# Transposing f, q and k by transfers instead of on TensorE, from the sixth unit on

**The chip, the cores and the metric.** One core of one Trainium2 chip. The metric is the device time of one execution in microseconds (us), lower is better. The median of three runs before was 474.9 us (472.83 to 475.72); later calls repeated the kernel before many times, with medians of 471.9 to 473.9. One core only, so a run counts as slow only when it is over 1.5% above the fastest of its kernel.

## The reference

A gated recurrence over 768 steps for 4 batches of 8 heads of 48 elements, then LayerNorm and a two-layer perceptron on the 384 concatenated elements. Cut to what matters:

```python
f = 1.0 / (1.0 + np.exp(-f_logit))               # q, k, v, f_logit: (4, 8, 768, 48) fp32
for t in range(S):
    state = f[:, :, t, :, None] * state + einsum('bhd,bhe->bhde', k[:, :, t], v[:, :, t])
    y[:, :, t] = einsum('bhd,bhde->bhe', q[:, :, t], state)
x = y.transpose(0, 2, 1, 3).reshape(B, S, H * D)
xn = (x - mu) / sqrt(var + 1e-6) * g_ln
out = x + maximum(xn @ w_ch1, 0.0) @ w_ch2       # 384 -> 1536 -> 384
```

## The kernel before

The 768 steps are cut into 12 units of 64. Inside a unit the recurrence becomes matrix products: f goes through a sigmoid and two running products along time (VectorE scans `after` and `upto`), k is multiplied by `after`, q by `upto`, and TensorE (PE) does the rest. The kernel runs the scans with time along the free axis, the inputs arrive with time on partitions, so f, k and q of each unit are transposed, eight 128 x 128 pieces each, on PE:

```python
def across(src, g):
    pt = one_bank(f"tr{n}")
    for a in range(NP):                                   # NP = 4, and g = 0, 1
        nc.tensor.transpose(pt[:, a * P:(a + 1) * P],
                            src[:, g, 2 * a:2 * a + 2].rearrange("p h e -> p (h e)"), ident)
    return pt.rearrange("p (s t) -> p s t", t=T)

def times(dst, pts, by):                                  # VectorE, 128 x 512 out of PSUM
    for g, pt in enumerate(pts):
        segs = slice(g * HS, (g + 1) * HS)
        nc.vector.tensor_tensor(out=dst[:, segs], in0=pt, in1=by[:, segs, 1:E1], op=ALU.mult)
...
    # do_gates, for g in 0, 1
    pt = across(loaded[n, "f"], g)
    nc.scalar.activation(out=gv[:, segs, 1:E1], in_=pt, func=AF.Sigmoid)
...
    # do_q; do_k is the same with k and "after"
    times(new("qh", [P, NS, T]), [across(loaded[n, "q"], g) for g in range(G)], at["upto"])
```

The order of all work is one string of tokens. A start-up string `START` brings in the weights and the first units; then a string `UNIT` is run for m = 3 to 11. In it `m{m}` is one piece of the perceptron of unit m (block products of 0.9 us on PE, or second-layer products of 1.95 us), `a{n}.name` a stage of the recurrence of unit n, `l{p}q` a load, `y` and `s` sums on VectorE that prepare the perceptron's products. A turn of this loop handles the perceptron of one unit and stages of three later ones:

```python
UNIT = """
a{o}.after m{m} m{m} m{m} m{m} m{m} a{n}.carried a{n}.scores a{n}.causal m{m} m{m} a{n}.chunk
a{n}.values m{m} a{n}.stats m{m} m{m} a{n}.norm m{m} m{m} m{m} m{m} m{m} s{m}
m{m} a{n}.turn a{o}.kx a{o}.k m{m} m{m} m{m} a{o}.kt a{p}.gates a{o}.upto l{p}v m{m}
l{z}f m{m} y{n} a{o}.q l{p}q a{n}.state a{o}.kept l{p}x l{p}k m{m}
"""
```

`carried`, `scores`, `chunk` and `values` matter later: each is 64 small products, which PE passes through in about one microsecond (0.93 to 1.08 us in the chain of the first trace).

## Time and profile before

| | before |
|---|---|
| median of 3 runs | 474.9 us |
| span of the profiled run, mean granted clock | 469.3 us, 0.989 |
| PE, VectorE (DVE), ScalarE (ACT), GpSimd (POOL) busy | 96%, 71%, 32%, 24% |
| one clean turn of the loop | 35.79 us |
| PE records of transposes of f, q, k | 3 x 96 = 288 |

The second is a row of the queues (queue and kind: packets, megabytes, share of the engines' time), one of two whose kind is "instruction", some 16 KB a packet:

```profile
q8 instruction: 46, 0.75, 0.6%
```

### The profile page before, as it was taken

How to read it: one execution, taken by the hardware profiler on the slowest of the kernel's cores; microseconds unless marked ns; L12 is line 12 of the kernel's file. 1: busy time of each engine (PE TensorE's matmuls, PEld its weight loads, DVE VectorE, ACT ScalarE, POOL GpSimd, SP SyncE). 2: the span in 40 equal slices, each digit the busy share in tenths (PEclk: the TensorE clock that was granted, in tenths of full speed). 3: DMA queues.
4: the chain of work that ended last, by engine and by line, in shares of the span. 5: the costliest groups of instructions: out<-in, count | busy, mean ns of one | idle time of the engine just before them, and what ended most of it. 6: DMA issues, size and time to landing. Idle time of an engine off the chain costs nothing.

```text
span 469.3 us, 13084 instructions
## 1 busy us (share of the span) xinstructions
PE 451.7 (96%) x5651; PEld 421.8 (90%) x5651; DVE 334.5 (71%) x543; ACT 149.3 (32%) x298; POOL 113.0 (24%) x110
## 2 busy tenths in 40 slices
PE   6689999999999999999999999999999999999994
PEld 5568886668999999999999999999999999999994
DVE  6796889437588676966967967867867867765561
ACT  2464752003313251242153143143143143141320
POOL 3223446079222013013004004004003003102010
PEclk9998999999999999999999999999999999999998
DMA  8999981264351502512522522522421410100001
GB/s 156 192 207 277 231 203 36 46 125 81 74 93 38 104 6 52 107 32 44 103 45 43 98 49 43 97 51 43 93 53 40 77 40 10 27 3 14 21 10 33
DMA packets 125969, 36.32 MB, mean 77 GB/s; under 512 B 116432, under 2 KB 122064, under 8 KB 125904
## 3 DMA queue, kind: packets, MB, share of 16 engines
q1 hardware_dynamic: 124128, 35.02, 36.1%
q8 instruction: 46, 0.75, 0.6%
q10 hardware_dynamic: 1776, 0.40, 0.4%
q14 instruction: 19, 0.16, 0.1%
HBM read 30.67 MB, written 4.72 MB: 75 GB/s over the span
## 4 chain that ended last, share of the span: by engine, by line
PE 91%; DMA 4%; SPq 2%; DVE 1%; issue 0%; ACT 0%
PE pp L935 29%; PE bx L844 11%; PE ph L906 9%; PE by L844 9%; PE po L916 7%; PE tr L611 6%; PE bz L844 3%; PE py L689 3%; PE py L729 2%; PE pn L759 2%; PE ps L703 2%; PE kp L719 2%; SPq L428 2%; PE bv L844 2%; PE bw L844 2%; PE xp L792 2%
## 5 line engine op out<-in xcount | busy, mean ns | idle before, releaser
L855 ACT ACTIVATE h<-h 128x512 f32<-128x512 f32 x45 | 28.4, 630 | 71.8 <-DVE h L852 64.9
L906 PE MATMUL ph<-xt,w 128*128 128x256 f32 x216 | 48.4, 381 | 0.0
L906 PEld LDWEIGHTS ph<-xt,w 128*128 128x128 f32 x216 | 40.4, 190 | 5.5
L747 POOL TENSOR_SCALAR rstd<-mv 128x2 f32<-128x2 f32 x12 | 2.8, 235 | 165.6 <-DVE mv L746 165.5
L935 PE MATMUL pp<-w,h 128*128 128x192 f32 x240 | 42.5, 328 | 0.0
L935 PE MATMUL pp<-mixed,h 128*128 128x192 f32 x240 | 42.4, 327 | 0.0
L935 PE MATMUL pp<-mixed,s 128*128 128x192 f32 x240 | 40.6, 326 | 0.0
L935 PEld LDWEIGHTS pp<-mixed,s 128*128 128x128 f32 x240 | 39.3, 190 | 0.0
L935 PEld LDWEIGHTS pp<-mixed,h 128*128 128x128 f32 x240 | 38.8, 190 | 0.1
L935 PEld LDWEIGHTS pp<-w,h 128*128 128x128 f32 x240 | 38.6, 190 | 0.2
L619 DVE TENSOR_TENSOR_SCAN after<-gates,ends 128x1040 f32<-128x1040 f32 (+1 forms) x13 | 28.6, 2198 | 5.2 <-ACT gates L648 5.2
L943 POOL TENSOR_TENSOR p1x<-p,x 128x192 f32<-128x192 f32 x10 | 13.8, 1376 | 76.1 <-ACT p L950 76.1
L916 PE MATMUL po<-w,h 128*128 128x384 f32 x96 | 32.0, 488 | 0.0
L631 DVE TENSOR_TENSOR_SCAN upto<-gates,starts 128x1040 f32<-128x1040 f32 (+1 forms) x13 | 30.3, 2334 | 0.4
L844 PE MATMUL bx<-y,v 128*128 128x128 f32 x216 | 30.1, 282 | 0.5 <-issue 0.5
L916 PEld LDWEIGHTS po<-w,h 128*128 128x128 f32 x96 | 17.9, 190 | 11.5
L852 DVE TENSOR_TENSOR h<-h,by 128x512 f32<-128x512 f32 x36 | 24.7, 686 | 5.0 <-PE by L844 2.9
L721 ACT COPY kt<-kp 128x512 f32<-128x512 f32 x24 | 13.0, 590 | 46.6 <-PE kp L719 46.6
L844 PEld LDWEIGHTS bx<-y,v 128*128 128x128 f32 x216 | 26.3, 191 | 1.2 <-issue 0.7
L745 DVE BATCH_NORM_STATS2 stats<-x 128x6 f32<-128x384 f32 x24 | 13.0, 543 | 19.5 <-ACT x L736 19.5
L849 ACT ACTIVATE h<-bw 128x512 f32<-128x512 f32 x9 | 5.4, 597 | 62.4 <-PE bw L844 62.4
L707 DVE TENSOR_TENSOR sc<-ps,causal 128x1024 f32<-128x1024 f32 x12 | 14.6, 1220 | 11.8 <-PE ps L703 11.8
(153 smaller groups left out, 969.8 us busy)
## 6 DMA issues: line engine op xcount, KB each, us to landing
w_0words<-in_moe_w_ch_dram SPq DMA_DIRECT2D x7, 768.0 KB, 5.5
kraw<-in_k_dram SPq DMA_DIRECT2D x48, 96.0 KB, 3.5
qraw<-in_q_dram SPq DMA_DIRECT2D x48, 96.0 KB, 3.1
v<-in_v_dram SPq DMA_DIRECT2D x48, 96.0 KB, 2.9
fraw<-in_f_logit_dram SPq DMA_DIRECT2D x46, 96.0 KB, 3.0
vx<-in_v_dram SPq DMA_DIRECT2D x48, 48.0 KB, 3.0
out_dram<-p1x SPq DMA_DIRECT2D x19, 48.0 KB, 2.0
out_dram<-u4y SPq DMA_DIRECT2D x19, 48.0 KB, 2.0
```

What stands on the lines that cost most here:

```text
L611: nc.tensor.transpose(pt[:, a * P:(a + 1) * P], src[:, g, 2 * a:2 * a + 2].rearrange("p h e -> p (h e)"), ident)
L619: nc.vector.tensor_tensor_scan(out=at["after"].rearrange(flat)[:, c0:c1][:, ::-1], data0=gt[:, c0 + 1:c1 + 1][:, ::-1], data1=ends.rearran ...
L631: nc.vector.tensor_tensor_scan(out=at["upto"].rearrange(flat)[:, c0:c1], data0=gt[:, c0:c1], data1=starts.rearrange(flat)[:, c0:c1], initi ...
L689: nc.tensor.matmul(py[half(b), r, e * D:(e + 1) * D], lhsT=qh[head_rows(r), 2 * e + b], rhs=kept[head_rows(r), b, e], start=e == 0, stop=F ...
L707: nc.vector.tensor_tensor(out=new("sc", [P, 2, GA, T]).rearrange("s r e t -> s (r e) t"), in0=at["ps"].rearrange("s r e t -> s (r e) t"), ...
L844: nc.tensor.matmul(banks[bank][:, i], lhsT=right[:, i * P:(i + 1) * P], rhs=left, start=new and i == 0, stop=True, skip_group_check=True)
L852: nc.vector.tensor_tensor(out=out[to], in0=out[to], in1=bank, op=op)
L855: nc.scalar.activation(out=out[to], in_=out[to] if bank is None else bank, func=AF.Relu)
L906: nc.tensor.matmul(ph[:, j], lhsT=w1[:, m, (i + j) * P:(i + j + 1) * P], rhs=xt[:, m], start=m == 0, stop=m == KD - 1)
L916: nc.tensor.matmul(po, lhsT=h[:, i, g * P:(g + 1) * P], rhs=w2[:, i], start=i == 0, stop=i == KF - 1)
L935: nc.tensor.matmul(pp, lhsT=a[:, i], rhs=b[:, i], start=i == 0, stop=i == KH - 1)
L943: engine.tensor_tensor(out=to, in0=x1, in1=x2, op=op)
```

## The change

The intent: take f, q and k off PE for units 5 to 11 and let transfers do the transposing. A transposing transfer is used here on two-byte elements, so ScalarE first splits each fp32 tensor into two planes of 16-bit halves, GpSimd's queue writes the planes to DRAM, and the queue of SyncE (SP) reads them back transposed, both halves side by side, so that the bits of an fp32 value meet again. The sigmoid and the two products then read SBUF. The core of the diff (`START`, comments, names and the dispatch of the new tokens cut; `DIRECT = 5`):

```diff
+    def split(n, name, g):                       # token p{n}{name}{g}
...
+        planes = raws.tile([P, 2, 64 * H], U16, tag="planes", name=f"{name}planes{n}_{g}")
+        nc.scalar.copy(
+            out=planes,
+            in_=raw_of(n, name)[:, g].rearrange("p h e -> p (h e)").bitcast(U16).rearrange(
+                "p (c two) -> p two c", two=2))
+        nc.gpsimd.dma_start(out=halved[n, name][g], in_=planes)
+
+    def transfer(n, name):                       # token x{n}{name}
...
+        if not turned:
+            turned["k"] = wide_heads["q"]...
+            turned["f"] = turned["q"] = late["pool"].tile([P, NS, T], FP32, name="turned")
+        there = halved.pop((n, name))
+        for g in range(G):
+            to = turned[name].rearrange("p (g s) t -> p g (s t)", g=G)[:, g].bitcast(U16)
+            nc.sync.dma_start_transpose(out=to.rearrange("p (a r) -> p a r", a=NP),
+                                        in_=there[g].rearrange("p two c -> (p two) c"))
...
-    gates = []
-    for i in range(2):
...
+    gates = consts.tile([P, NS * E1 + 1], FP32)
...
-        nc.tensor.matmul(one_bank("idle")[:, 0:2 * P], lhsT=nothing, ...
+        nc.tensor.matmul(one_bank("idle")[:, 0:2 * P], lhsT=ident, ...
...
+            if n >= DIRECT:
+                nc.scalar.activation(out=gv[:, :, 1:E1], in_=turned["f"], func=AF.Sigmoid)
+                return
...
+                nc.vector.tensor_tensor(out=qh, in0=turned["q"], in1=at["upto"][:, :, 1:E1],
+                                        op=ALU.mult)   # k likewise
...
 UNIT = """
-a{o}.after m{m} m{m} m{m} m{m} m{m} a{n}.carried a{n}.scores a{n}.causal m{m} m{m} a{n}.chunk
-a{n}.values m{m} a{n}.stats m{m} m{m} a{n}.norm m{m} m{m} m{m} m{m} m{m} s{m}
-m{m} a{n}.turn a{o}.kx a{o}.k m{m} m{m} m{m} a{o}.kt a{p}.gates a{o}.upto l{p}v m{m}
-l{z}f m{m} y{n} a{o}.q l{p}q a{n}.state a{o}.kept l{p}x l{p}k m{m}
+a{o}.after m{m} m{m} a{n}.carried a{n}.scores p{o}q0 m{m} a{n}.causal m{m} m{m} m{m} p{o}q1
+l{p}k m{m} a{n}.values a{o}.upto a{n}.chunk a{n}.stats m{m} x{o}q p{p}f0 m{m} m{m} m{m}
+m{m} m{m} x{o}k m{m} m{m} p{p}k0 p{p}k1 a{n}.norm s{m} m{m} l{p}x m{m}
+a{o}.q p{p}f1 l{p}q x{p}f m{m} a{n}.turn a{o}.k m{m} m{m} y{n} l{p}v m{m}
+a{p}.gates l{z}f a{n}.state m{m} a{o}.kept a{o}.kt
 """
```

Two side effects. One tile of gates serves all units where there were two, and the raw k tile now takes q as well.

More of the change, by code (lines that the diff above doesn't have):

```diff
@@ L11 @@
 U32 = mybir.dt.uint32
+U16 = mybir.dt.uint16
 AF = mybir.ActivationFunctionType
@@ L305 @@
 START = """
-d l0k l0q a0.gates a0.after d f a0.upto r l0x l0v f
-a0.kx d l1f d a0.k a0.kept d d l1k a0.q d a0.carried
-a0.scores l1x a0.causal a0.values r w f f l1q a0.stats d a0.kt
-l1v f w a1.gates a0.norm a1.after a0.chunk a0.turn a0.state a1.kx r a1.upto
-m0 a1.kept w a1.k m0 a1.q f r l2v a1.kt a1.carried w
-d f a1.scores l2k f r a1.causal m0 w f a1.values r
-r a1.chunk a1.stats l2f m0 w f l2x m0 a1.norm a1.turn r
-w m0 r r w a1.state m1 m1 f m1 m1 a2.gates
-m1 w w l2q a2.after r a2.kx w f r w l3k
@@ L315 @@
-a2.k a2.upto a2.kept m0 m1 m0 a2.q m0 m0 m0 m0 l3q
-l3v l3f a2.carried a2.scores U m1 a2.causal l3x a2.values U m1 a2.stats
-a2.norm m1 m1 m1 m1 T a3.gates a2.kt a2.turn a2.chunk U a3.kx
-a3.after a3.k a3.upto U l4f m2 a2.state l4k U a3.kept m2 a3.q
-m2 m2 a3.carried a3.scores U U a3.causal U l4v t U a4.gates
-a3.kt a3.values T a4.after a3.chunk a3.state U m2 l4q a3.stats m2 U
-a3.norm l5v s2 m2 a4.kx l5f l5k m2 m2 a4.k a4.upto m2
-U a5.gates a4.q m2 a4.kt a3.turn l4x u l5q y3 l5x a4.kept
-l6f m2 m2
+a0.gates l0k l0q f d a0.after l0x d r l0v d a0.upto
@@ new lines @@
+d f a0.kx l1f a0.k a0.kept l1k d a0.q f a0.carried a0.scores
+a0.causal a0.values l1x l1q w r d a0.stats a0.kt f a1.gates w
+d d a0.norm d a1.after l1v a0.chunk a0.turn f a0.state a1.upto m0
+a1.kept r w a1.kx f a1.k m0 a1.q f r a1.kt r
+w a1.carried a1.scores a1.causal d f l2k f l2v f w m0
+a1.values r a1.stats l2f r a1.chunk w m0 a1.norm d l2x m0
+a1.turn r m0 m1 r w w f w r m1 w
+l2q m1 a1.state m1 a2.gates a2.after r m1 a2.kx f m0 m0
+r w a2.k l3k w a2.upto a2.kept m1 a2.q m0 m0 m0
+m0 a2.carried l3q a2.scores l3v l3f m1 l3x a2.causal U a2.values a2.stats
@@ L324 @@
+a2.norm m1 m1 m1 a3.gates m1 m1 a2.kt a2.turn a2.chunk a3.kx m2
+m2 l4f a3.after a3.k m2 U a3.upto U T a2.state U a3.q
+a3.kept m2 a3.carried a3.scores a3.kt l4v l4k a3.causal U a4.gates U U
+U l4q T t U a3.values a3.chunk a4.after m2 l5f l5v U
+a3.stats m2 a4.kx U a3.norm s2 m2 p5f0 a3.state l5k m2 a4.k
+U m2 p5f1 m2 a4.kt u a3.turn l6f x5f p5k0 a4.upto a4.q
+l4x p5k1 y3 l5q a5.gates m2 m2 l5x a4.kept m2
 """
 UNIT = """
-a{o}.after m{m} m{m} m{m} m{m} m{m} a{n}.carried a{n}.scores a{n}.causal m{m} m{m} a{n}.chunk
@@ L372 @@
     FIRST = 3
+    DIRECT = 5
     PIECE = 768
@@ L408, with raw_of @@
     loaded = {}
+    turned = {}
+    drams = fast.enter_context(tc.tile_pool(name="drams", bufs=2, space=bass.MemoryType.DRAM))
+    halved = {}
+    def raw_of(n, name):
+        return wide_heads["k" if n >= DIRECT and name == "q" else name]
+    def split(n, name, g):
+        if n >= NU or n < DIRECT:
+            return
+        if (n, name) not in halved:
+            halved[n, name] = drams.tile([G, P, 2, 64 * H], U16, tag=f"{name}halves",
+                                         name=f"{name}halves{n}")
+        planes = raws.tile([P, 2, 64 * H], U16, tag="planes", name=f"{name}planes{n}_{g}")
[5 more added lines that the diff above has]
+    def transfer(n, name):
+        if n >= NU or n < DIRECT:
+            return
+        if not turned:
+            turned["k"] = wide_heads["q"].rearrange("p g h e -> p (g h e)").rearrange(
+                "p (s t) -> p s t", t=T)
+            turned["f"] = turned["q"] = late["pool"].tile([P, NS, T], FP32, name="turned")
[4 more added lines that the diff above has]
+                                        in_=there[g].rearrange("p two c -> (p two) c"))
     def load(n, name, engines=(nc.sync,)):
@@ L424, in load @@
         else:
-            loaded[n, name] = wide_heads[name]
+            loaded[n, name] = raw_of(n, name)
         src = {"f": f_logit, "k": k, "q": q, "v": v}[name]
@@ L454 @@
     nc.vector.memset(starts, 0.0)
-    gates = []
-    for i in range(2):
-        t = consts.tile([P, NS * E1 + 1], FP32, name=f"gates{i}")
-        nc.gpsimd.memset(t, 0.0)
-        gates.append(t)
+    gates = consts.tile([P, NS * E1 + 1], FP32)
+    nc.gpsimd.memset(gates, 0.0)
     least = consts.tile([P, NS], FP32)
@@ L530 @@
     to_mix = list(range(0, KH, 2))
-    nothing = consts.tile([P, P], FP32)
-    nc.vector.memset(nothing, 0.0)
     def idle():
-        nc.tensor.matmul(one_bank("idle")[:, 0:2 * P], lhsT=nothing,
-                         rhs=nothing.unsqueeze(1).broadcast_to([P, 2, P]), start=True, stop=True)
+        nc.tensor.matmul(one_bank("idle")[:, 0:2 * P], lhsT=ident,
+                         rhs=ident.unsqueeze(1).broadcast_to([P, 2, P]), start=True, stop=True)
     def mix(engine=nc.vector):
@@ L595, in attention @@
     def attention(n):
-        gt = gates[n % 2]
+        gt = gates
         gv = gt[:, 0:NS * E1].rearrange("p (s e) -> p s e", e=E1)
@@ L644, in do_gates @@
             new("total", [P, NS], bufs=2)
+            if n >= DIRECT:
+                nc.scalar.activation(out=gv[:, :, 1:E1], in_=turned["f"], func=AF.Sigmoid)
+                return
             for g in range(G):
@@ L661, in do_k_across @@
         def do_k_across():
-            at["pk"] = [across(loaded[n, "k"], g) for g in range(G)]
+            if n < DIRECT:
+                at["pk"] = [across(loaded[n, "k"], g) for g in range(G)]
         def do_k():
-            times(new("kh", [P, NS, T]), at["pk"], at["after"])
-        def do_q():
-            times(new("qh", [P, NS, T]), [across(loaded[n, "q"], g) for g in range(G)],
-                  at["upto"])
+            kh = new("kh", [P, NS, T])
+            if n < DIRECT:
+                times(kh, at["pk"], at["after"])
+            else:
+                nc.vector.tensor_tensor(out=kh, in0=turned["k"], in1=at["after"][:, :, 1:E1],
+                                        op=ALU.mult)
+        def do_q():
+            qh = new("qh", [P, NS, T])
+            if n < DIRECT:
+                times(qh, [across(loaded[n, "q"], g) for g in range(G)], at["upto"])
+            else:
+                nc.vector.tensor_tensor(out=qh, in0=turned["q"], in1=at["upto"][:, :, 1:E1],
+                                        op=ALU.mult)
             nc.vector.tensor_tensor(out=least, in0=least, in1=at["total"], op=ALU.min)
@@ L998, in run @@
                 load(int(rest[:-1]), rest[-1])
+            elif kind == "p":
+                split(int(rest[:-2]), rest[-2], int(rest[-1]))
+            elif kind == "x":
+                transfer(int(rest[:-1]), rest[-1])
             elif kind == "s":
```

## The prediction

> **What bounds the kernel now.** I read the page's busy shares and slices first, then the chain that ended last, then the stretches of one repetition of the steady loop, then PE, SP and ACT in order of time inside that repetition. The totals and slices of the page:
>
> ```profile
> PE 451.7 (96%) x5651; PEld 421.8 (90%) x5651; DVE 334.5 (71%) x543; ACT 149.3 (32%) x298; POOL 113.0 (24%) x110
> ...
> PE   6689999999999999999999999999999999999994
> ...
> ACT  2464752003313251242153143143143143141320
> ...
> DMA  8999981264351502512522522522421410100001
> ...
> PE 91%; DMA 4%; SPq 2%; DVE 1%; issue 0%; ACT 0%
> ```
>
> The PE row is 9 from the fourth slice to the last but one, and 91% of the chain is PE. A busy PE alone proves little, since ends of matmuls are modelled, so the stretches matter more. Each row below is start and end, length, then busy time of PE, PEld, DVE, ACT and POOL with counts, granted clock, DMA share and GB/s:
>
> ```profile
> 0.00:100.00 100.00, 89.70 (x975) 70.31 (x976) 75.75 (x100) 39.61 (x67) 36.62 (x37) 0.97 0.75 166
> ...
> 308.24:344.03 35.79, 35.79 (x505) 35.35 (x499) 27.15 (x47) 11.48 (x24) 6.06 (x6) 1.00 0.32 63
> ...
> 421.40:469.30 47.90, 41.72 (x294) 41.10 (x293) 22.07 (x43) 9.38 (x20) 6.21 (x8) 0.97 0.08 19
> ```
>
> The middle row is one turn of the unit loop: 35.79 us, PE without a gap, DVE 76%, ACT 32%, POOL 17%, DMA 32%. Idle PE lies at the start (100 - 89.70 = 10.3 us, waits for the first loads and weights) and at the end (6.2 us). Between them any PE work taken out shortens the kernel one for one, until something else becomes late. The three transposed inputs in that turn, in order of time on PE (start, us, engine, line, operands, count):
>
> ```profile
> 317.44 0.82 PE L792 MATMUL xp<-ident,xn 128*128 128x128 f32 x6
> 318.10 1.04 PE L611 MATMUL tr<-ident,kraw 128*128 128x128 f32 x8
> 318.97 2.15 PE L935 MATMUL pp<-w,h 128*128 128x192 f32 x12
> ...
> 325.73 1.04 PE L611 MATMUL tr<-ident,fraw 128*128 128x128 f32 x8
> 326.61 2.12 PE L935 MATMUL pp<-mixed,h 128*128 128x192 f32 x12
> ...
> 330.51 1.04 PE L611 MATMUL tr<-ident,qraw 128*128 128x128 f32 x8
> 331.38 2.12 PE L935 MATMUL pp<-mixed,h 128*128 128x192 f32 x12
> ```
>
> What eight transposes cost is the distance to the next start, not their durations: 318.97 - 318.10 = 0.87, 326.61 - 325.73 = 0.88, 331.38 - 330.51 = 0.87. The busy sum of the same 24 instructions (24 x 0.273 = 6.6 us) would overstate it.
>
> [...] The trace's median is 273 ns[...]; eight of them pipelined cost 0.87 us, 109 ns each, and that is what I use. [...] the u4y addition on POOL takes 2.61 us beside a VectorE scan of 2.44 us, while the same-size u4x addition takes 0.59 us.
>
> **The change part by part.** (1) PE. Units 5 to 11, seven of twelve, lose the 24 transposes: 0.87 + 0.88 + 0.87 = 2.62 us per unit, 7 x 2.62 = 18.3 us. All of these transposes lie between about 150 and 402 us, where PE has no gap. The order of PE's other work changes but not its amount; the start gets two more idle matmuls of about 0.31 us (two took 0.63 us in the chain). The loop's turn should fall to 35.79 - 2.62 = 33.17 us.
>
> (2) ScalarE gets, per unit, six splits of 128 x 1024 two-byte elements. From the measured 923 ns for 768 strided elements[...] one is about 1.13 us: 6.8 us. Two gate sigmoids of 608 ns become one of about 1.1 us. ACT goes from 11.5 to 18.2 us of 33.2, 55%. That is hidden as a total; each split can delay an eviction behind it by about 1 us, while the four single PSUM banks give some cover, and the six banks a turn that the transposes took are no longer asked for.
>
> (3) VectorE. Per unit four products out of PSUM (2 x 678 + 2 x 680 ns = 2.7 us) become two of 128 x 1024 out of SBUF. The causal product of that size takes 1.22 us, so 2.4 us. DVE stays near 27 us of 33.2, 81%; still not the bound.
>
> (4) Transfers. Per unit six writes to HBM and six transposing reads, each 128 x 2048 bytes = 256 KB, so 1.57 MB each way. The fullest slice moved 277 GB/s, so the writes need an estimated 5.7 us of all engines[...]. The old traffic took 0.32 x 35.79 = 11.5 us. Sum 23.2 of 33.2 us, 70%. A single path is: split 1.1, write about 3, transposing read about 3 to 4 us (estimates from the landing times of 3 us that 96 KB loads show[...]). SP is the queue that starts them:
>
> ```profile
> 329.40 1.16 SPq L948 DMA_DIRECT2D out_dram<-u4y  x2
> 330.66 2.72 SPq L428 DMA_DIRECT2D fraw<-in_f_logit_dram  x4
> ...
> 334.79 2.72 SPq L428 DMA_DIRECT2D qraw<-in_q_dram  x4
> ```
>
> An issue costs 2.72 / 4 = 0.68 us, and one turn has about 19.6 us of them. Six more at that size make 23.6 of 33.2 us: fits, if a transposing issue is not much dearer than a plain one.
>
> (5) Do they come in time? Laying the new token order out on PE (0.9 us per block product, 1.95 us per product of the second layer): q's second split falls at about 9 us into the turn, is in HBM at about 13, back transposed at about 17 to 19; its product stands at about 22. k's halves were written in the turn before; its read follows q's and ends near 21, needed near 25. f is tightest: second split at about 21, written at 25, and its read can start only when q's product has freed the shared tile (23.5), so it lands near 30. The sigmoid stands at about 30.5, and VectorE's next scan at 33.2. What would hurt PE is later still: ACT's next evictions are those of k at 33 and of the next turn's first products, so I count some 4 us of slack.
>
> Sum: 474.9 - 18.3 + 0.6 (idle matmuls, if they lie on the path) + about 1.5 for scattered waits and for the first hand-over at unit 5, where the pipeline of transfers is filled = 458.7, say 459 us. The median is of unprofiled runs; the saving is taken from the profiled one, whose span is 1.2% shorter.
>
> **The rivals.** First, late data becomes the bound: ACT stands at the gates' sigmoid until f arrives, evictions pile up behind it and PE starves. For it: the path split, write, read passes three queues[...]. Against: slack as laid out, and about 30% of DMA time free. If each turn lost 2 us, 7 x 2 = 14 us come back and the result is about 472, same; at 4 us a turn, 487, slower. Second, the transposing transfers are far slower [...]. [...] Nothing in the old profile speaks to it, because it holds no such transfer. [...] Fourth, the reordered start gains: part of the 10.3 idle us before 100 us could close, 2 to 3 us, giving 456; it could as well lose that much.
>
> **Range and chances.** The PE term is firm, the lateness terms are all one-sided upwards, and the order of tokens looks laid out by someone who knew the latencies. So: 459 us, range 453 to 478. Faster by over 2% means below 465.4: 0.70, which needs less than about 1 us lost per turn. Within 2% (a loss of 1 to 4 us per turn): 0.17. Slower by over 2% (transfers or SP become the bound): 0.13.
>
> **What would show it right or wrong.** Right: PE groups of tr shrink from 288 to 120 instructions; the distance between the same product in successive turns is near 33.2 us and PE has no gap in it; splits near 1.1 us and ACT near 55% in a turn; DMA share near 0.7; the six transposing transfers land in 3 to 5 us. Wrong: waits of ACT at the sigmoid on a transfer followed by PE waits for ACT; SP busy through the whole turn; a DMA share of 0.9 or more in the loop; POOL late with its writes; a VectorE product waiting for q or k; or splits at 2 us and more, which would put ACT near 24 us of 33.

## More of the kernel before

The page and the stretches are shown in the prediction. Two views that it does not show turn out to matter. The first lists PE's waits, longest sums first: the line that waited, what it waited for, us in total, times, longest. These two stand well down the list:

```profile
PE py L729 <- issue: 0.7, 1, 0.7
...
PE bx L844 <- issue: 0.5, 1, 0.5
```

"issue" means a wait for which the profile shows no releaser at all.

## The result, and the profile after

The kernel after takes 451.81 us (median of 4 runs, 449.57 to 452.71), against 473.87 us (median of 4 runs, 471.49 to 475.72) of the kernel before in the same rounds: a ratio of 0.953, interval 0.947 to 0.959. Ratios here are the mean time of one kernel's fast runs over that of the other's of the same rounds, so they are not quite the ratio of the medians. The direction and the mechanism of the prediction hold; the time lies 1.2 us below its range.

The page of the kernel after: busy shares, the PE, ACT and DMA slices, and the shares of the chain that ended last.

```profile
PE 433.4 (96%) x5487; PEld 402.7 (89%) x5487; DVE 328.2 (73%) x528; ACT 186.1 (41%) x333; POOL 120.7 (27%) x151
...
PE   5699999999999999999999999999999999999994
...
ACT  2446754003134545455454454464464451341320
...
DMA  8997888063645867787879776796788550000001
...
PE 90%; DMA 4%; DVE 3%; ACT 1%; SPq 1%; issue 1%; POOL 0%; POOLq 0%; ACTq 0%; DVEq 0%
```

PE is still the bound from the fourth slice on. It lost 18.3 us of busy time (451.7 to 433.4); that this equals the 18.3 us predicted is partly chance, because 168 transposes of 0.27 us would be 46 us of durations, of which most overlap. The DMA slices of the loop went from mostly 1 to 5 up to mostly 5 to 9.

Three turns of the loop after, each from the first second-layer product to the next one's (start and end, length, then busy us and count of PE, PEld, DVE, ACT, POOL, then granted clock, DMA share, GB/s):

```profile
169.75:202.98 33.23, 33.23 (x477) 32.68 (x476) 26.86 (x45) 16.59 (x30) 7.48 (x12) 1.00 0.80 165
202.98:236.21 33.23, 33.23 (x477) 32.68 (x475) 26.75 (x45) 16.62 (x30) 7.48 (x12) 1.00 0.79 156
236.21:269.44 33.23, 33.23 (x476) 32.68 (x475) 26.86 (x45) 16.59 (x30) 6.82 (x12) 1.00 0.84 173
```

The same three turns before, in the first trace:

```profile
171.27:207.81 36.54, 36.05 (x501) 35.42 (x499) 27.16 (x47) 11.48 (x25) 6.06 (x6) 1.00 0.32 61
207.81:243.80 35.99, 35.99 (x501) 35.49 (x500) 27.16 (x47) 11.53 (x25) 6.07 (x6) 1.00 0.32 62
243.80:279.59 35.79, 35.79 (x501) 35.36 (x500) 27.16 (x47) 11.47 (x25) 6.06 (x6) 1.00 0.32 62
```

Read the second column. After, every turn is 33.23 us, with PE never idle. Before, the clean turn is 35.79, but the first turns are longer. The clean turns differ by 35.79 - 33.23 = 2.56 us, and seven of them make 17.9 us; the prediction had 18.3. PE's idle time ahead of the loop did not move: in both traces the same work of PE ends at 129.37 us, with 119.07 us busy before and 119.17 after. ScalarE's 16.6 us of 33.2 (50%), VectorE's 26.8 (81%) and a DMA share of 0.79 to 0.84 are what the other engines got.

So 17.9 us of about 22 are the transposes. The search below is mostly for the remaining three to four.

**The path of f.** The tile into which f and q are transposed, with what it waits for and who waits for it (engine and line, operation, count: duration in ns min/median/max, first and last start):

```profile
L449 SPq DMA_TRANSPOSE turned<-fhalves x14: 1232/1253/2134, 144.8 to 347.5; - x14
L449 SPq DMA_TRANSPOSE turned<-qhalves x14: 1226/1322/2569, 164.9 to 364.9; - x14
...
  ACT gates L682: 44.0, 7
```

A transposing transfer holds SP's queue 1.25 to 1.32 us, not 0.68; k's take 1.44 us in the median. The seven sigmoids wait 44.0 us for f, 6.3 each. ScalarE's own timeline shows one of them, and SP's the two transfers it waits for (start us, us, engine, line, operands, count; in brackets the idle time before and its releaser):

```profile
208.49 1.05 ACT L432 COPY fplanes<-fraw 128x1024 uint16<-128x1024 uint16 x1 [1.74 <-issue]
...
219.23 1.06 ACT L682 ACTIVATE gates<-turned 128x1024 f32<-128x1024 f32 x1 [8.11 <-DMA turned<-fhalves]
```

```profile
213.19 2.63 SPq L449 DMA_TRANSPOSE turned<-fhalves  x2
215.91 2.22 SPq L997 DMA_DIRECT2D out_dram<-u4y  x2
218.22 2.72 SPq L470 DMA_DIRECT2D v<-in_v_dram  x4
```

Split at 208.5, transposing reads issued from 213.2, data at 219.2. The first block product of the next turn starts at 218.27, so f is 1.0 us later than that, and ScalarE's evictions behind it come late (that of the first block product starts at 221.14). PE still does not wait: up to that eviction it starts on bx, py and ps (at 219.16, 220.15 and 221.12 us). The 8.11 us of idle ScalarE look alarming and cost nothing, but little of the slack is left.

### The profile page after: what moved, and what is told of

Same layout as the page of the kernel before. It is cut to its first block, busy times and chain, and to the rows that moved or that the text cites.

```text
span 450.2 us, 13028 instructions
## 1 busy us (share of the span) xinstructions
PE 433.4 (96%) x5487; PEld 402.7 (89%) x5487; DVE 328.2 (73%) x528; ACT 186.1 (41%) x333; POOL 120.7 (27%) x151
## 4 chain that ended last, share of the span: by engine, by line
PE 90%; DMA 4%; DVE 3%; ACT 1%; SPq 1%; issue 1%; POOL 0%; POOLq 0%; ACTq 0%; DVEq 0%
PE pp L984 30%; PE bx L893 12%; PE by L893 9%; PE ph L955 9%; PE po L965 6%; PE bz L893 4%; PE py L778 3%; PE py L738 3%; PE ps L752 3%; PE pn L808 2%; PE kp L768 2%; PE tr L647 2%; DMA fraw<-in_f_logit_dram 2%; PE bv L893 2%; PE bw L893 2%; PE xp L841 2%
## 5 line engine op out<-in xcount | busy, mean ns | idle before, releaser
L984 PE MATMUL pp<-mixed,s 128*128 128x192 f32 x240 | 42.0, 326 | 0.0
L984 PE MATMUL pp<-w,h 128*128 128x192 f32 x240 | 40.7, 326 | 0.0
L436 POOL DMA_DIRECT2D qhalves<-qplanes x14 | 7.7, 547 | 99.9 <-ACT qplanes L432 99.9
L901 DVE TENSOR_TENSOR h<-h,bx 128x512 f32<-128x512 f32 x27 | 18.5, 686 | 18.2 <-PE bx L893 18.2
L682 ACT ACTIVATE gates<-turned 128x1024 f32<-128x1024 f32 x7 | 7.4, 1058 | 44.0 <-DMA turned<-fhalves 44.0
L843 ACT ACTIVATE xt<-xp,gain 128x128 f32<-128x128 f32 x72 | 19.9, 378 | 11.1 <-PE xp L841 11.1
L559 POOL TENSOR_TENSOR w<-w_0upper,w_0units 128x768 int32<-128x768 int32 x7 | 12.7, 1818 | 32.6 <-DVE w_0upper L557 27.6
```

The costliest lines, as they stand in the source:

```text
L843: nc.scalar.mul(out=xt[:, m, g * P:(g + 1) * P], in_=pt[:, m], mul=gain[:, m:m + 1])
L901: nc.vector.tensor_tensor(out=out[to], in0=out[to], in1=bank, op=op)
L984: nc.tensor.matmul(pp, lhsT=a[:, i], rhs=b[:, i], start=i == 0, stop=i == KH - 1)
```

## The experiments

Each is an edit of one of the two kernels, shown as a short diff; all gave correct results unless said. What was expected was written before each run, and names theories as they stood then.

### The unaltered kernel, and the two start-ups

The first rival was my fourth: the rewritten start gains (or loses) a few us. Three runs on one chip, with the kernel before at 473.32 us (median of 19 runs): the kernel after unaltered, the kernel before with the new `START` (tokens for the split and the transfer taken out), and the kernel after with the old `START`, to whose tail those tokens are added.

> The changed kernel unaltered, as the control on this chip. The profiles account for 19.1 us (18.3 of transposes and 0.8 to 1.2 of small waits in the first loop turns of the old kernel), the first medians for 22.1. If the missing 3 us are chance in the few runs of the old kernel: its median here comes out at 471 to 472 and the changed one 19 us below it. If the change really gives 22: 22 again.

> The old kernel with only the new order of the start (no transposing transfers, old unit loop, 36 transposes per repetition as before). If the reordered start gives what my sum lacked: 3 to 4 us faster than the old kernel, about 0.992. If the start gives nothing: 1.000 within 0.003. If the new start only pays with the transfers: 1.000 or above.

```diff
 # e1: before.py
-START = """ d l0k l0q a0.gates a0.after d f a0.upto ... l6f m2 m2 """
+START = """ a0.gates l0k l0q f d a0.after l0x d r ... l5x a4.kept m2 """   # no p5*, no x5*
```

> The changed kernel with the old order of the start and the five hand-over tokens put in near its end. If the transposes taken off TensorE are nearly the whole gain: 18.3 to 19.5 us faster than the old kernel, 0.959 to 0.961. If the start carries 3 to 4 us of the gain: as said, 0.960, while the changed kernel is at 0.953. If the start gives nothing and the loop gives more than the transposes: 0.953 as the changed kernel.

```diff
 # e2: after.py, with the old START and this tail
+... l5k m2 p5f0 p5f1 x5f m2 a4.k a4.upto m2
+U a4.q m2 a4.kt a3.turn l4x u p5k0 p5k1 l5q y3 a5.gates l5x a4.kept
+l6f m2 m2
```

Measured: 451.95 us (ratio 0.9555, interval 0.951 to 0.960) for the kernel after again; 473.28 (1.002, 0.9995 to 1.005) for the new start alone; 452.79 (0.9575, 0.953 to 0.962) for the old start under the new loop. The new start alone gives wrong values, because in it the load of f for unit 6 stands before the gates of unit 5 have read the shared tile; only its time is used. The start carries about 452.79 - 451.95 = 0.8 us of the gain (the intervals of these two overlap), and none under the old loop. That rival falls, and all but a sliver of the gain is in the loop.

### A second trace of the kernel before

> The old kernel unaltered, for a second trace of it. One theory of the 3 us that the 18.3 us of transposes leave open: the old unit loop loses 1 to 4 us per run in waits of TensorE that name no releaser, so its first turns are longer than 35.79 us (36.5 and 36.0 in the first trace; 37.5, 36.9 and 36.1 with the new start), while the changed loop's turns are 33.23 us from the first on. Rival: the excess lies ahead of the loop, before 130 us, and differs from run to run in both kernels; then the turns here are 35.79 us throughout in a run that is longer than 471 us.

475.56 us, one run. The same three turns as above:

```profile
173.40:211.04 37.64, 36.06 (x501) 35.43 (x499) 27.17 (x47) 11.47 (x25) 6.06 (x6) 1.00 0.32 59
211.04:247.59 36.55, 36.25 (x501) 35.56 (x499) 27.18 (x47) 11.53 (x25) 6.07 (x6) 1.00 0.32 61
247.59:283.38 35.79, 35.79 (x501) 35.35 (x499) 27.17 (x47) 11.48 (x25) 6.06 (x6) 1.00 0.33 62
```

The clean turn is the same 35.79, but the first turns are longer still. Summed from the turns shown on, what lies above the clean turn is 0.95 us in the first trace of before, 3.03 in this one and 3.06 in the run with the new start alone. The loop's very first turn, ahead of these, has such a wait too: 0.7 us in the first trace of before, 0.9 in this one, none with the new start. Together that is 1.7, 3.9 and 3.1 us, 2.9 in the mean. In three traces of the new loop (after, after again, after with the old start) the turns lose 0, 0.3 and 0, and the very first turn 0, 0.4 and 0.6: 0.4 in the mean. Part of the chain that ended last in this second trace of before:

```profile
201.19 0.93 PE py L729 x64
202.12 0.42 PE bx L844 x2
202.54 1.58 issue
204.13 0.94 PE bx L844 x6
```

PE has passed through two times 128 small products with only two block products between, begins the next block product, and stands for 1.58 us with nothing to wait for. Counting PE's records from 0 in the order of their starts (products, weight loads, and the few dozen records of its sequencer), every such wait in the loops, of both kernels, begins at a number that leaves 193 when divided by 256: 3777 and 4801 in the first trace of before, 3777, 4801 and 5825 in this one. Each ends 1.3 to 1.5 us after a transfer of the instruction queue has landed (the wait that ends at 163.77 us in the first trace of before: a packet landed at 162.25). Hence a new theory: PE has run ahead of its own instruction stream, which would come in blocks of 256 records, with a border after each. Three figures speak for it: the period of 256 in the numbers at which the waits begin, the 16 KB of a packet, and the count of packets, 46 for 11,381 records of PE in the first trace of before and 45 for 11,034 after, one for about 246. That these packets hold PE's instructions is inferred from this, and how PE takes them up is not shown. The waits are 0.3 to 1.6 us each.

### Is it the numbering? Shifted instructions in both kernels

If so, moving the block borders moves the waits. In the kernel before each idle product of the start was replaced by 19 small ones (648 more instructions ahead of the loop), so that the borders fall elsewhere; in the kernel after 30 small products were added to move its border into its quick stretch.

> The old kernel with 648 more instructions on TensorE's queue in the idle slots of the start (19 small products in place of each wide idle product), nothing else changed. In all traces so far TensorE's waits without a releaser begin at its instructions 3777, 4801 and 5825, 1024 apart, and only where one of these lies at the end of the 512 quick instructions of the attention's small products; each ends 1.2 to 1.5 us after an instruction fetch lands. If fetching of instructions is the cause: with 648 more these numbers fall before the quick stretch, the waits vanish, the unit loop's turns are 35.79 us from the first on and the kernel is 1 to 3 us faster, 0.994 to 0.998. If the cause lies in the work of those turns (late transfers, settling of buffers): the first turns stay at 36.5 us and more.

```diff
-        nc.tensor.matmul(one_bank("idle")[:, 0:2 * P], lhsT=nothing, ...)
+        for i in range(19):          # r = c = i % 2, one 64 x 64 by 64 x 48 product each
+            nc.tensor.matmul(bank[64 * r:64 * r + 64, i // 2 * D:(i // 2 + 1) * D],
+                             lhsT=nothing[64 * c:64 * c + 64, 0:64],
+                             rhs=nothing[64 * c:64 * c + 64, 0:D], start=True, stop=True)
```

> The changed kernel with 60 more TensorE instructions in the first idle slot, so that its instruction 4801 falls 2 after the end of a quick stretch instead of 62 after it. If instruction fetch is the cause: a wait of 0.5 to 1.6 us at instruction 4801, near 196 us, which the changed kernel does not have, and 0 to 2 us more in all. If not: no such wait.

```diff
 # in idle(), at its first call only
+            for j in range(30):
+                nc.tensor.matmul(... ident[64 * c:64 * c + 64, 0:64] ... ident[..., 0:D] ...)
```

The first took 478.1 us (1.012, interval 1.007 to 1.017): slower, where it was expected to be faster. Its first turns are 35.79, 35.86 and 35.79, as the theory said. But a wait of 3.9 us came up during the start, and later turns of 37.34 and 36.45, again all at numbers of the same remainder. The waits moved with the numbering, and the total got worse: the mechanism was supported and my forecast of the sum was a miss. The second took 454.06 (0.963). Its aim failed: each such product leaves four records, so 120 instructions were added where I had meant 60, and nothing can be read from it.

### Is it the length of the quick stretch? Spread in the old loop, together in the new

The theory in its sharper form: a border costs time when PE takes some 512 instructions in a quick run, and the two pieces `m` (2.0 us) between the small products of the old loop give the fetch too little time; the five of the new one (4.9 us) give enough. So the old loop was spread, and the new one drawn together.

> The old kernel with its chunk and values products three block products later in the unit loop, so that the two quick stretches of 256 TensorE instructions stand 81 instructions apart in place of 33, as in the changed kernel. Numbers of instructions stay. If the length of the quick stretch is what outruns the fetching: no waits without a releaser at 4801 and 5825, turns of 35.79 us from the first on, and 1.5 to 2.5 us less, 0.995 to 0.997. If the shorter turn's other drift is what helps the changed kernel: waits as before, 1.000.

```diff
 # before.py, UNIT
-... a{n}.carried a{n}.scores a{n}.causal m{m} m{m} a{n}.chunk
-a{n}.values m{m} a{n}.stats m{m} m{m} a{n}.norm m{m} m{m} m{m} m{m} m{m} s{m}
+... a{n}.carried a{n}.scores a{n}.causal m{m} m{m} m{m} m{m} m{m}
+a{n}.chunk a{n}.values a{n}.stats m{m} m{m} a{n}.norm m{m} m{m} m{m} s{m}
```

> The changed kernel with its values and chunk products three block products earlier, so that the quick stretches stand 33 instructions apart as in the old one. If the length of the quick stretch matters: waits without a releaser appear where a number that leaves 193 falls near the end of a stretch: at 6593 (4 after the end, near 261 us), 0.5 to 1.6 us, perhaps at 3777 and 9409 too, and 1 to 3 us more than the changed kernel. If not: none, and the time of the changed kernel.

```diff
 # after.py, UNIT
-... p{o}q0 m{m} a{n}.causal m{m} m{m} m{m} p{o}q1
-l{p}k m{m} a{n}.values a{o}.upto a{n}.chunk a{n}.stats ...
+... p{o}q0 m{m} a{n}.causal m{m} a{n}.values a{n}.chunk m{m} m{m} p{o}q1
+l{p}k m{m} a{o}.upto a{n}.stats ...
```

The spread old loop took 472.98 us (1.002, interval 0.9996 to 1.004), and no wait of its loop is without a releaser. The time did not fall, since the new order costs 0.36 us in every turn (36.15 against 35.79): the waits went and something else of the same size came. The new loop drawn together took 467.6 (0.992): most of the loss is VectorE's, which now comes late for PE once a turn. PE's waits, as above:

```profile
PE by L893 <- DVE h L901: 11.9, 7, 1.7
...
PE by L893 <- issue: 1.9, 1, 1.9
```

The second line is the point. The wait without a releaser is back in a loop that had none this long, and it stands at instruction 6593, the number named beforehand, right behind the small products. A shorter one, 0.3 us, stands at 9153; at 3777 and 9409, named as possible, there is none:

```profile
263.73 1.08 PE py L778 x64
264.80 0.93 PE pn L808 x64
265.74 1.90 issue
267.64 1.17 PE by L893 x8
```

So, in one trace of each, distance took these waits out of the old loop and closeness brought one back into the new. What is not settled: why a border inside a spread stretch sometimes still costs 0.4 to 0.6 us (one wait each in the second trace of after and in the trace with the old start), and whether the number of the border or the pause before it matters more in a given turn. No law that forecasts the sum came out.

### How much slack the path of f has

Theory: late data are hidden by some 4 us of slack. The transposing reads of f were started one piece of work later, then after the loads of v.

> The changed kernel with f's transposing transfer started two second-layer products later in SP's order, about 2 us later. If there are some 4 us of slack, as the prediction counted: no change, 1.000 to the changed kernel. If the slack is under 2 us (ACT already reaches the evictions behind the sigmoid 1.8 us late): up to 1 us per turn, 7 us in all.

```diff
-a{o}.q p{p}f1 l{p}q x{p}f m{m} a{n}.turn a{o}.k m{m} m{m} y{n} l{p}v m{m}
+a{o}.q p{p}f1 l{p}q m{m} a{n}.turn a{o}.k m{m} m{m} x{p}f y{n} l{p}v m{m}
```

> The same with f's transfer behind the loads of v, about 5 us later. With 4 us of slack: about 1 us per turn, 5 to 8 us in all. With under 2 us of slack: 3 to 4 us per turn, 20 to 28 us, so that the whole gain is gone. If lateness of f does not reach TensorE at all: unchanged.

```diff
+a{o}.q p{p}f1 l{p}q m{m} a{n}.turn a{o}.k m{m} m{m} y{n} l{p}v x{p}f m{m}
```

455.33 us (0.964, interval 0.958 to 0.971), turns about 34.0: the sigmoids waited 57.2 us in place of 44.0, that is 1.9 us more each, and 0.8 us of it reached the turn. Then 486.25 (1.028, 1.022 to 1.034), turns of 38.2 to 41.0, the sigmoids waiting 82.2 us, or 5.5 us more each than in the kernel after. The sigmoid's line in the two traces, as above:

```profile
  ACT gates L682: 57.2, 7
```

```profile
  ACT gates L682: 82.2, 7
```

In the second run PE waits for what stands behind the sigmoid on ScalarE:

```profile
PE bv L893 <- ACT kt L770: 24.4, 6, 5.4
```

That is my first rival, in flesh: ScalarE stands at the sigmoid, the copy of kt behind it is late, and PE starves. It is real, it just did not happen in the kernel as given. From the first of the two, 1.9 us of lateness minus 0.8 that showed leaves about 1.1 us of slack, not 4.

### The inner loop of the split

> The changed kernel with ScalarE's splits running pair by pair (inner loop of 2 elements, reading in order, writing to the two planes in turn) in place of 512 elements of one plane. If ScalarE's time goes by elements alone: splits stay at 1.05 us and the time is that of the changed kernel. If each short inner run costs extra: splits of 2 us or more, ACT above 22 us of a 33 us turn, f's second half late, and 5 us or more lost in all.

```diff
-            out=planes,
+            out=planes.rearrange("p two c -> p c two"),
...
-                "p (c two) -> p two c", two=2))
+                "p (c two) -> p c two", two=2))
```

556.63 us (1.175, interval 1.166 to 1.183). The same copy of the same elements, only with the two halves as the inner loop in place of the 512 elements of a plane. The group of the splits of f in the kernel after, then in this run (operands, count, busy us, mean ns of one, idle before and releasers):

```profile
L432 ACT COPY fplanes<-fraw 128x1024 uint16<-128x1024 uint16 x14 | 14.5, 1042 | 12.2 <-issue 10.3 <-DMA khalves<-kplanes 1.9
```

```profile
L432 ACT COPY fplanes<-fraw 128x1024 uint16<-128x1024 uint16 x14 | 66.3, 4772 | 0.0
```

1.04 us against 4.77. Six splits a turn cost 28.6 us in place of 6.3, ScalarE becomes the bound and turns grow to between 44.6 and 50.3 us. The order of the copy is not a detail: with the halves inside, the change loses 17%. The edit changes two things at once, though: the inner loop is shorter, and each write jumps from one plane to the other. Which of the two costs the time no run separates.

### Who starts the writes, and an earlier start

> The changed kernel with the six writes of the halves started by SP instead of GpSimd. SP has about 31 of 33.2 us of a turn taken in the changed kernel. If SP's queue is the next bound: 6 x 0.7 = 4 us more, so turns of 35 us and more and 12 to 20 us lost. If SP's time is mostly waiting that can overlap: about the changed kernel's time.

```diff
-        nc.gpsimd.dma_start(out=halved[n, name][g], in_=planes)
+        nc.sync.dma_start(out=halved[n, name][g], in_=planes)
```

458.61 us (0.971, interval 0.967 to 0.976), turns between 33.23 and 35.26. It costs some 7 us of the gain, fewer than expected: SP has little left to give, but a little.

> The changed kernel with the transfers from the fifth unit on instead of the sixth (one more unit; order in the start moved for it). If PE's own work sets the time wherever it has no gap: 2.6 us below the changed kernel. If the start's transfers (weights still being fetched and opened on ScalarE and GpSimd) leave no room there: no gain, with PE waits on the fifth unit's products between 130 and 160 us.

> The transfers from the fifth unit on, with the order mended where the first attempt lost 14 us: there the fifth unit's gates stood on ScalarE in front of the copy of the third unit's values, waiting for a transfer, and all behind it was late. Here the gates come after it and the halves are written earlier. If the fifth unit can be hidden with room: 2.6 us below the changed kernel. If the weights' mixing on GpSimd, whose queue also starts the writes, leaves no room: again slower than the changed kernel, with waits of TensorE between 130 and 170 us.

```diff
-    DIRECT = 5
+    DIRECT = 4
 # START, its last five lines, first order; the second order moved a4.gates later
+m2 l4f a3.after a3.k m2 U l4k a3.upto U T p4f0 p4f1 a2.state U a3.q
+a3.kept m2 x4f p4k0 p4k1 a3.carried a3.scores a3.kt l4v l4q a3.causal U x4k U U a4.gates
...
```

466.17 us (0.985, 0.981 to 0.990) and 469.09 (0.994, 0.992 to 0.996). One more unit off PE should have given 2.6 us and lost 14 and 17 instead. The turns of the loop are the same 33.23; the loss is ahead of it. PE's longest wait in the first of the two:

```profile
PE pp L984 <- DVE s L873: 9.0, 1, 9.0
```

There GpSimd still mixes weights: the chain that ended last goes through its additions from 126 to 142 us, then through the normalisation to the sums `s` that PE waited for. The first write of q's halves also stood behind these additions (split at 136.6, write issued at 139.4 us), and ScalarE waited 5.8 us at the sigmoid of unit 4 while other copies stood behind it. Which of these costs most no run separates. The second order made the wait of 9.0 us one of 12.2. I did not find an order that beats the kernel after.

## Why the prediction was right or wrong

*What bounds the kernel.* Right in the main: PE is all but without a gap in the loop, before and after, and work taken from it there shortened the kernel. But "where PE has no gap" overlooked 0.67 us at 163.1 and 0.49 at 200.4 in its own trace.

*(1) PE.* Right in kind, 2% too high: 2.56 us per turn in place of 2.62, 17.9 in place of 18.3. Taking the distance to the next start and not the durations was what made it so close. The idle matmuls, +0.6 us, were put on the path; the start shows no loss, so that term measured 0.

*(2) ScalarE and (3) VectorE.* The splits took 1.04 us for 1.13 predicted (the step from the 923 ns of 768 elements to 1,024 was an estimate of mine), the sigmoid 1.06, the products 1.21 for 1.22, ScalarE's turn 16.6 for 18.2, VectorE's share 81% as said. Right that none of it reaches PE.

*(4) Transfers.* The landing times of 3 to 4 us hold in the median for f and k (3.6), not for q (4.8); the DMA share is 0.8 where I had 0.70, a sum in which the part of the transposing reads was an estimate of mine that no trace had shown. The issue was sized wrong: 1.25 to 1.44 us for 256 KB, where the working took the 0.68 us of a plain load of 96 KB. The condition I had attached to it, "if a transposing issue is not much dearer than a plain one", did not hold: SP's queue is taken for 27 to 29 of 33.2 us, summed over its own timeline, where I had 23.6. Yet SP did not become the bound.

*(5) Slack.* Wrong in size. I had the sigmoid at 30.5 us after the turn's first block product; it came at 34.2 (219.23 against a first block product at 185.04). "Some 4 us of slack" was about 1. The time lost nothing by it, but one piece of work more would have cost, as the first delay of f's read shows.

*The sum: the step that failed.* "474.9 - 18.3 + 0.6 (idle matmuls, if they lie on the path) + about 1.5 for scattered waits and for the first hand-over at unit 5" predicts a saving of 16.2 us. Measured in one call it is 473.3 - 451.95 = 21.4. Term by term:

| term | in the prediction | measured |
|---|---|---|
| transposes off PE | -18.3 | -17.9 |
| idle matmuls | +0.6 | 0 |
| scattered waits, first hand-over | +1.5 | 0 |
| turns above the clean one and waits without a releaser, old loop against new | absent | -2.9 + 0.4 = -2.5 |
| the new start | a rival of 2 to 3 either way | 0 to -0.8 |
| sum | -16.2 | -20.4 to -21.2 |

0.2 to 1.0 us is left, which runs that scatter over 2 us (450.69 to 452.95) cover. Besides, the base of 474.9, the median of three runs, was 1.6 us above the median of 19. Two things were mis-sized together: the 2.1 us of allowance for losses that did not come, and the missing 2.5 us that the old loop itself lost and the new one does not. That is also where the range failed. "The lateness terms are all one-sided upwards" holds for the new kernel alone; it forgot that the old kernel has waits of its own, which a new order can take away. I had even seen them in the list, as 0.7 and 0.5 us, and took the clean turn of a run whose time, 471.1 us, was 3.8 us under the median that I subtracted from (0.8%; the 1.2% in the prediction sets a span against a time). The waits differ from trace to trace (1.7 to 3.9 us over the loop), so a single trace could not have sized them; a note that the first turns were 36.54 and 35.99 long in place of 35.79 could have.

*The rivals.* Late data as the bound: not in the kernel as given, but shown by starting f's read later. Far slower transposing transfers: no, they land in 3.3 to 7.5 us. POOL late with its writes: no loss per turn is seen; POOL is busy 7.5 of 33.2 us, and a write holds it 0.54 to 0.59 us in the median. The start gains: about 0.8 us at most, within the noise.

What is shown and what is argued: that the waits follow the numbering in 256s and the closeness of the small products is shown by the shifted, the spread and the drawn-together loops, one trace of each, while the time of the spread loop did not fall. That they are instruction fetches rests on the period and on the 16 KB packets that land 1.3 to 1.8 us before each ends in all these traces; no run here changes the fetch itself. The 2.5 us are a difference of turns and waits in three traces of each loop; that the new order brings them is argued from those runs. That the 2.56 us of a clean turn are the transposes rests on the 2.62 us that they took: no run takes them out and keeps the old order.

## What to carry to other kernels

When one engine has no gap, work out a saving from the distance between successive starts in a turn, then ask for both kernels what the turns lose beyond the clean one, and read it in more than one trace, with base and saving from the same runs. A wait that names no releaser is not noise (0.3 to 1.6 us each in the old loop): count the instructions, and try long runs of tiny products further apart (in the old loop that took the waits away, but not the time). Before work is moved to an engine with time to spare, look at the order in which it reads and writes (a factor of 4.6 here) and at the one queue that starts most transfers (27 to 29 of 33.2 us taken): this kernel stands about 1 us from being bound by f's path.
